# A sum of products by seven instead of eight in the last stage, a new order for the second half, and products of zeros at the start

## The chip, the cores and the metric

The kernel runs on one core of a Trainium2 chip. The metric is the device time of one execution in microseconds (us): the median of three timed runs is 601.54 us, from 601.0 to 602.06. A profile of one further execution goes with them.

The engines by their short names: PE (TensorE) multiplies matrices and writes its sums into PSUM; DVE (VectorE), ACT (ScalarE) and POOL (GpSimd) work on tiles in SBUF, the first two also on PSUM; SP's queue issues most transfers (DMA), and ACT's and POOL's queues issue some.

## The reference

Causal attention of 4 batches x 12 heads, 448 tokens, head size 64, and then on its output an MLP with a squared ReLU, 1792 tokens wide in all, from 768 to 2048 and back to 768:

```python
scores = scale * np.matmul(q, k.transpose(0, 1, 3, 2))       # (4, 12, 448, 448)
scores = np.where(np.triu(ones, k=1), -1e9, scores)
attn = softmax(scores)                                       # over the last axis
x = np.matmul(attn, v).transpose(0, 2, 1, 3).reshape(1792, 768)
h = np.maximum(x @ w_in, 0.0)                                # (1792, 2048)
out = h * h @ w_out                                          # (1792, 768)
```

All is float32. The kernel gets that precision from fast products by writing each factor as a high and a low part; each product of blocks is then three matmuls (high x high, high x low, low x high).

## The kernel before

**Attention** goes by pairs of heads (`attention`). Tiles named a... and b... belong to two pairs that take turns: aq, ak are loaded, transposed on DVE to aqt, akt (line 351); PE makes the scores (line 380); DVE masks them and finds the row extremes (line 393), ACT takes the exponentials into ap (line 397), POOL or DVE divides by the sums (lines 406, 408), PE transposes the result (line 422) to apt, and multiplies it with v (line 464).

**The MLP of the first half** of the tokens (896) is done plainly: h products (`h_unit`, lines 662 to 664), the square, o products (`o_unit`, lines 1081 to 1083). They fill PE between the products of attention.

**The MLP of the second half** works on 2x2 blocks with seven products in the place of eight, Winograd's form: the keys are 11, 12, s1 to s4 and 22, and each has a factor of sums and differences on both sides. d_ff is cut into four groups, taken in the order `TURNS = (0, 3, 2, 1)`. For each group there are two h stages (`h_pair(gr, u, ...)`, u = 0, 1; lines 843 to 847) and one o stage (`o_seven`; lines 969 to 971). A stage works on banks of PSUM; a bank is emptied by ACT (line 266, r<-ps) or by DVE as an add into the running sum of the outputs (line 269, sb<-ps,sb and sa<-ps,sa). DVE, ACT and POOL also make the factors of the next stage from h (the `less`, `square` and `factor` steps), among them sums of two SBUF tiles (r<-r,r; g<-r,g). The factors of the weights are derived once per group by `added_up`: loads, scalings, and transfers from POOL's queue that add into the tile in SBUF. Weights that are already split into high and low parts are loaded by line 944 for the o stages (wi<-wo_split) and by line 783 for the h stages.

**The last o stage** (`o_last`) is plain: four blocks, three column groups (d), and for each four products, so that nothing is left to add up afterwards; the last group's h stages are plain in their last step as well (`plain`). Each output block of 448 tokens is transposed on DVE and stored (lines 1019, 1024); the very last one by PE (`finish`, lines 1046 to 1061), which begins when PE has ended its last product.

**The order.** All instructions are first recorded as operations in a list, with the tiles they take and give back. `PLACES`, a table of base-36 numbers, gives each operation its place in the program and which engine does it where there is a choice (number modulo 3). `emit` then issues the operations in that order. A bank of PSUM or a buffer goes to the next operation that asks for one, the one that was given back first by the program's order. So an engine waits where its next instruction, in this order, isn't ready.

Of the kernel before, what the change touches and what calls it, by code (L numbers as in the profile page):

```python
# [130 lines left out]
def kernel(  # L131
# [85 lines left out]
    def tiles(nm, n, shape, dtype, pool=const):  # L217
        return [pool.tile(shape, dtype, name=f"{nm}{i}") for i in range(n)]

    early = ExitStack()  # L220
# [5 lines left out]
    x_t = tiles("x", NA, [P, 2, S], F32R)  # L226
# [15 lines left out]
    NX = 9  # L242
    wide = wi_t.rearrange("p i c f -> p (i c f)")
# [46 lines left out]
    vs = {}  # L290

    def attention(s, n, at):
# [74 lines left out]
        def softmax(chunks, at):  # L367
# [7 lines left out]
            def scores():  # L375
                for c in chunks:
# [7 lines left out]
            plan.op(at, [(PE, 0.16 + sum(2 * CW[c] / 2400 + 0.01 for c in chunks), scores)],  # L384
                    [(nm, "qt"), (nm, "kt")] + [(nm, "kd")] * any(c in FIRST for c in chunks), holds, take=holds,
                    clear=[(nm, "p", c) for c in chunks], lag=spare(0.6))
# [201 lines left out]
    def piece(rank, kind, gr, a, ch, after):  # L588
# [96 lines left out]
    x7 = {}  # L685
# [144 lines left out]

    def h_pair(gr, u, W, rank, step, plain):

# [4 lines left out]
        def product(key, b, begin):  # L837
            nonlocal rank
            ps, w = bank[b], W[key]
            for c in range(CB):  # L840
                def go(c=c):
# [7 lines left out]
                plan.op(rank, [(PE, 3 * t_mm(S), go)],  # L849
                        [(w, 0), (w, 1)] + [(("x7", OTHER[key], c), i) for i in range(2)], [ps],  # L850
                        take=ps if begin and c == 0 else None, drop=[w])
# [30 lines left out]
        factor("11", "11", plain)  # L882
# [10 lines left out]
        factor("22", "u3", plain)  # L893
# [4 lines left out]
        factor("21", "21", plain)  # L898
# [4 lines left out]
        if plain:  # L903
            factor("12", "12", True)
            return rank
# [18 lines left out]
    O_BANK = {"11": "a", "12": "a", "s3": "d", "s1": "c", "s2": "b", "22": "d", "s4": "c"}  # L924
    O_ENDS = ("12", "s2", "22", "s4")
# [3 lines left out]
    def o_parts(gr, rank, last):  # L929

        W, Z, gate = {}, {}, list(ahead)

        def at(key, u):
            return rank + (last - rank) * (SEVEN.index(key) + u / 2) / 7
# [4 lines left out]
        for m, key in enumerate(("11", "12", "22") if gr != TURNS[-1] else ("11", "12", "21", "22")):  # L939
# [7 lines left out]
        for u in range(2):  # L947
# [8 lines left out]
            if gr != TURNS[-1]:  # L956
                added_up(rank, CH, source, done, lambda t: t, True)
# [48 lines left out]
    def o_last(W, rank, step):  # L1006

        for k in ("11", "21", "12", "22"):
            i, j = k
            for d in range(CB):  # L1010
                ps, a = Hold("ps", "os"), o_sum(k, d)
                rank = o_product(ps, [(W[i + m, u], g7[TURNS[-1], m + j, u]) for m in "12" for u in range(2)],
                                 d, True, True, rank, step)
                if (k, d) == ("22", CB - 1):
                    finish(ps, a, d, rank)
                    continue
                plan.op(rank, [on_dve(S, a, lambda ps=ps: ps.t[:, :S], a, ALU.add)], [ps], [("sum", k, d)], drop=[ps])
                h = Hold("f", "tr")
                plan.op(rank, [(DVE, t_dve(S) + 0.05, lambda h=h, a=a: nc.vector.transpose(h.t, a()))],
                        [("sum", k, d)], [h], take=h)  # L1020
                row, col = T + (int(j) - 1) * S, (int(i) - 1) * CH + d * P
                for s in range(P // SQ):
                    def go(eng, h=h, s=s, row=row, col=col):
                        return lambda: eng.dma_start(
                            out=out[row:row + S, col + s * SQ:col + (s + 1) * SQ].rearrange(
                                "(b p) d -> p b d", p=SQ),
                            in_=h.t[s * SQ:(s + 1) * SQ].rearrange("p (b d) -> p b d", d=SQ))
# [331 lines left out]
```

## Time and profile before

| what | value |
|---|---|
| median of three runs | 601.54 us (601.0 to 602.06) |
| the profiled execution | 601.9 us |
| its span | 599.8 us, mean granted clock 0.995 |
| PE busy | 582.2 us (97%), 3718 instructions |
| DVE busy | 454.8 us (76%), 1077 instructions |
| ACT busy | 351.7 us (59%), 893 instructions |
| POOL busy | 274.5 us (46%), 378 instructions |
| matmuls of the last o stage | 144, each 128x448 |

The span is from the first to the last instruction of the program; the execution's own time lies 2.1 us above it. The trace counts a matmul as busy from its start to its modelled end, so that consecutive ones overlap (a matmul of 448 columns has a length of 0.36 us and follows the one before after about 0.2 us). The granted clock is given in shares of TensorE's full clock of 2.4 GHz.

### The profile page before, as it was taken

The page shows a single profiled execution, that of the slowest core. Times are in us where ns is not written, and L with a number is a line of the kernel's source. Part 1 is how long each engine was busy: PE and PEld are TensorE (multiplying, and loading weights), DVE is VectorE, ACT ScalarE, POOL GpSimd, SP SyncE. Part 2 cuts the span into 40 slices and gives each one's busy share as a digit, 9 for nine tenths or more (in the row PEclk, how much of TensorE's full clock was granted, in tenths as well). Part 3 has the DMA queues.
Part 4 walks back from the last instruction along what each step waited for, and adds up shares of the span by engine and source line. Part 5 has one row for each costly group of instructions (what it writes and reads, how often), then busy time and mean ns, then how long its engine had stood idle before and what let it go on. Part 6 is the DMA issues. An engine that isn't in the chain of part 4 may idle for free.

```text
span 599.8 us, 11359 instructions
## 1 busy us (share of the span) xinstructions
PE 582.2 (97%) x3718; PEld 510.0 (85%) x3718; DVE 454.8 (76%) x1077; ACT 351.7 (59%) x893; POOL 274.5 (46%) x378
## 2 busy tenths in 40 slices
PE   3899999999999999999999999999999999999997
PEld 2577778798988998988889889999999999999996
DVE  5999998688966898897798658577638758776674
ACT  3899987776756853767457442247565645633310
POOL 2566652243135352333224453654766566756310
PEclk9899999999999999999999999999999999999999
DMA  8888534999888987995899699867877766773556
GB/s 148 188 174 203 141 65 111 259 275 315 225 249 248 267 221 171 298 288 154 222 294 309 219 294 277 252 195 175 234 159 172 149 142 144 168 174 60 162 97 103
DMA packets 190650, 119.99 MB, mean 200 GB/s; under 512 B 126016, under 2 KB 178560, under 8 KB 190592
## 3 DMA queue, kind: packets, MB, share of 16 engines
q1 hardware_dynamic: 169488, 107.99, 64.4%
q0 software_dynamic: 6912, 9.44, 10.2%
q10 hardware_dynamic: 14192, 1.85, 1.9%
q8 instruction: 29, 0.48, 0.4%
q14 instruction: 29, 0.24, 0.1%
HBM read 80.71 MB, written 38.54 MB: 199 GB/s over the span
## 4 chain that ended last, share of the span: by engine, by line
PE 91%; ACT 3%; DMA 3%; DVE 1%; SPq 1%; issue 0%; POOL 0%; ACTq 0%
PE ps L1081 7%; PE ps L662 7%; PE ps L1083 7%; PE ps L1082 7%; PE ps L464 6%; PE ps L663 6%; PE ps L664 6%; PE ps L847 6%; PE ps L845 6%; PE ps L843 6%; PE ps L971 6%; PE ps L969 6%; PE ps L970 6%; PE ps L422 6%; PE ps L380 5%; ACT bp L397 1%
## 5 line engine op out<-in xcount | busy, mean ns | idle before, releaser
L266 ACT ACTIVATE words<-words 128x384 f32<-128x384 f32 (+3 forms) x128 | 73.6, 596 | 35.1 <-DVE words L269 11.4
L1081 PE MATMUL ps<-wo,g 128*128 128x384 f32 x224 | 77.3, 345 | 0.0
L393 DVE CUSTOM_DVE_ANT_0 ps<-ps,mask 128x64 f32<-128x64 f32 (+6 forms) x168 | 68.0, 444 | 11.1 <-PE ps L380 9.7
L1083 PE MATMUL ps<-wo,g 128*128 128x384 f32 x224 | 75.1, 335 | 0.0
L1082 PE MATMUL ps<-wo,g 128*128 128x384 f32 x224 | 75.1, 335 | 0.0
L397 ACT ACTIVATE ap<-ps,mx 128x256 f32<-128x256 f32 (+6 forms) x126 | 58.8, 479 | 26.4 <-DVE mx L393 25.5
L662 PE MATMUL ps<-x,wi 128*128 128x448 f32 x192 | 73.7, 384 | 0.0
L663 PE MATMUL ps<-x,wi 128*128 128x448 f32 x192 | 70.2, 365 | 0.0
L664 PE MATMUL ps<-x,wi 128*128 128x448 f32 x192 | 70.2, 365 | 0.0
L406 POOL TENSOR_SCALAR ap<-ap,asm 128x256 f32<-128x256 f32 (+6 forms) x80 | 43.0, 555 | 46.1 <-DVE asm L499 20.6
L970 PE MATMUL ps<-g,wi 128*128 128x448 f32 x153 | 56.0, 366 | 0.0
L971 PE MATMUL ps<-g,wi 128*128 128x448 f32 x153 | 56.0, 366 | 0.0
L969 PE MATMUL ps<-g,wi 128*128 128x448 f32 x153 | 56.0, 366 | 0.0
L273 POOL TENSOR_TENSOR wi<-words,wi 128x384 fp32r<-128x384 f32 (+1 forms) x38 | 45.7, 1227 | 21.4 <-ACT wi L266 20.6
L845 PE MATMUL ps<-x,wi 128*128 128x448 f32 x150 | 55.0, 367 | 0.0
L847 PE MATMUL ps<-x,wi 128*128 128x448 f32 x150 | 55.0, 367 | 0.0
L843 PE MATMUL ps<-x,wi 128*128 128x448 f32 x150 | 54.9, 366 | 0.0
L266 ACT ACTIVATE r<-ps 128x448 f32<-128x448 f32 x56 | 30.1, 542 | 35.5 <-PE ps L847 18.1
L269 DVE TENSOR_TENSOR g<-r,g 128x448 fp32r<-128x448 f32 x54 | 37.4, 703 | 11.1 <-ACT g L266 7.0
L266 ACT ACTIVATE r<-r 128x448 f32<-128x448 f32 x58 | 32.9, 574 | 17.8 <-DVE r L269 17.1
L1081 PEld LDWEIGHTS ps<-wo,g 128*128 128x128 f32 x224 | 42.1, 188 | 1.0 <-issue 0.4
L266 ACT ACTIVATE wi<-words 128x384 fp32r<-128x384 f32 (+1 forms) x53 | 28.5, 545 | 24.6 <-PE ps L970 8.5
(158 smaller groups left out, 1470.4 us busy)
## 6 DMA issues: line engine op xcount, KB each, us to landing
words<-in_moe_w_in_dram SPq DMA_DIRECT2D x24, 512.0 KB, 5.5
words<-in_moe_w_out_dram SPq DMA_DIRECT2D x32, 384.0 KB, 3.8
wo_split<-wo SPq DMA_DIRECT2D x26, 384.0 KB, 4.5
wi<-wo_split SPq DMA_DIRECT2D x22, 384.0 KB, 3.6
wo_whole<-words SPq DMA_DIRECT2D x32, 192.0 KB, 3.5
wi_split<-wi SPq DMA_DIRECT2D x24, 256.0 KB, 3.7
v<-in_v_dram SPq DMA_DIRECT2D x24, 192.0 KB, 4.0
wi_whole<-words SPq DMA_DIRECT2D x18, 256.0 KB, 4.0
```

Source lines behind the costliest of these rows:

```text
L266: return (ACT, t_act(n, psum, more), lambda: nc.scalar.activation(dst(), src(), func, **kw))
L662: nc.tensor.matmul(o, w[:, 0], x[:, 0], start=c == 0, stop=False)
L663: nc.tensor.matmul(o, w[:, 0], x[:, 1], start=False, stop=False)
L664: nc.tensor.matmul(o, w[:, 1], x[:, 0], start=False, stop=c == NP - 1)
L845: nc.tensor.matmul(o, w.t[:, 0, c], x[:, 1], start=False, stop=False, skip_group_check=True)
L847: nc.tensor.matmul(o, w.t[:, 1, c], x[:, 0], start=False, stop=c == CB - 1, skip_group_check=True)
L969: nc.tensor.matmul(o, w.t[:, 0, d], g.t[:, 0], start=start, stop=False, skip_group_check=True)
L970: nc.tensor.matmul(o, w.t[:, 0, d], g.t[:, 1], start=False, stop=False, skip_group_check=True)
L971: nc.tensor.matmul(o, w.t[:, 1, d], g.t[:, 0], start=False, stop=stop, skip_group_check=True)
L1081: nc.tensor.matmul(res(), g[:, 0], w[:, 0], start=f == 0, stop=False)
L1082: nc.tensor.matmul(res(), g[:, 0], w[:, 1], start=False, stop=False)
L1083: nc.tensor.matmul(res(), g[:, 1], w[:, 0], start=False, stop=f == GF - 1)
```

## The change

1. `o_last` makes the last o stage by the seven keys too (`O_LAST`): for each column group 7 keys x 2 halves x 3 matmuls, 126 in all. The results of keys that belong to more than one block are added to more than one running sum: DVE adds from PSUM 21 times in this stage, where it was 12. The last group's weights are now derived by `added_up` (on POOL's queue), and its h stages draw up the factors t1 to t4 as the others do (`plain` is gone).
2. Both h stages of the last group now come before the second-last o stage, and buffers that held the x factors are lent to the g factors and the weights when the last h stage is done with them (`lent_x`).
3. One x tile is set to zero at the start of DVE's queue, and `warmed` issues products of it whose result nobody reads: 15 ahead of the first scores, 7 and 3 among the first transposes.
4. `PLACES` is new. Apart from the zero products, the order of the first half is what it was; from the end of attention on, it is another.

On PE at the start, where akt, aqt, bkt, bqt are the transposed inputs, ap the probabilities of the first pair and x11 the zero tile. Before:

```order
L380 MATMUL ps0_113<-akt_69,aqt_68 64x320 x2
L380 MATMUL ps1_114<-akt_69,aqt_68 64x256 x2
...
L380 MATMUL ps6_119<-bkt_139,bqt_138 64x448 x2
L380 MATMUL ps7_120<-bkt_139,bqt_138 64x384 x2
L380 MATMUL ps7_120<-bkt_139,bqt_138 64x64 x2
L422 MATMUL ps0_113<-ident_64,ap_71 128x128 x4
L422 MATMUL ps2_115<-ident_64,ap_71 128x128 x4
L422 MATMUL ps3_116<-ident_64,ap_71 128x128 x4
```

After:

```order
L307 MATMUL ps0_114<-x11_72 128x448 x15
L398 MATMUL ps1_115<-akt_82,aqt_81 64x320 x2
...
L398 MATMUL ps0_114<-bkt_140,bqt_139 64x384 x2
L398 MATMUL ps0_114<-bkt_140,bqt_139 64x64 x2
L307 MATMUL ps1_115<-x11_72 128x448 x7
L440 MATMUL ps3_117<-ident_77,ap_84 128x128 x4
L307 MATMUL ps4_118<-x11_72 128x448 x3
L440 MATMUL ps2_116<-ident_77,ap_84 128x128 x4
L440 MATMUL ps1_115<-ident_77,ap_84 128x128 x4
```

The products of the zero tile stand ahead of the first scores, behind the second pair's scores, and between the first and the second group of transposes.

On PE in the second half, where h products (into ps banks, from x and weights wi) and o products (from g) interleave. Before, the h stage's bank ps2, between one sum and the next:

```order
L847 MATMUL ps2_115<-x2_8_3924,wi_91 128x448
L843 MATMUL ps7_120<-x2_81,wi_91 128x448
L845 MATMUL ps7_120<-x2_81,wi_91 128x448
L847 MATMUL ps7_120<-x2_81,wi_91 128x448
L843 MATMUL ps3_116<-x4_83,wi_91 128x448
L845 MATMUL ps3_116<-x4_83,wi_91 128x448
L847 MATMUL ps3_116<-x4_83,wi_91 128x448
L843 MATMUL ps2_115<-x6_85,wi_91 128x448
```

After, bank ps4 at the same stage of the program:

```order
L870 MATMUL ps6_120<-x7_68,wi_92 128x448
L866 MATMUL ps4_118<-x2_5_3947,wi_92 128x448
L868 MATMUL ps4_118<-x2_5_3947,wi_92 128x448
L870 MATMUL ps4_118<-x2_5_3947,wi_92 128x448
L866 MATMUL ps6_120<-x8_69,wi_92 128x448
L868 MATMUL ps6_120<-x8_69,wi_92 128x448
L870 MATMUL ps6_120<-x8_69,wi_92 128x448
L991 MATMUL ps4_118<-g3_96,w3_4368 128x448
```

Before, ps2 is used again seven products after the start of the last one of the old sum; after the change, ps4 is used again four products after.

On DVE at the end of the program, where sb5, sb8, sb9, sb10 and sb11 are running sums of output blocks and ps the banks. Before:

```order
L269 TENSOR_TENSOR sb5_4315<-ps5_118,sb5_4315 128x448
L1019 STREAM_TRANSPOSE words_96<-sb5_4315 128x448
L269 TENSOR_TENSOR sb9_4319<-ps2_115,sb9_4319 128x448
L1019 STREAM_TRANSPOSE words_96<-sb9_4319 128x448
L269 TENSOR_TENSOR sb10_4320<-ps3_116,sb10_4320 128x448
L1019 STREAM_TRANSPOSE words_96<-sb10_4320 128x448
L269 TENSOR_TENSOR sb11_4321<-ps0_113,sb11_4321 128x192
L269 TENSOR_TENSOR sb11_4321<-ps0_113,sb11_4321 128x256
```

After:

```order
L277 TENSOR_TENSOR sb11_4389<-ps4_118,sb11_4389 128x448
L277 TENSOR_TENSOR sb11_4389<-ps5_119,sb11_4389 128x448
L1052 STREAM_TRANSPOSE words_97<-sb11_4389 128x448
L277 TENSOR_TENSOR sb8_4386<-ps2_116,sb8_4386 128x448
L277 TENSOR_TENSOR sb5_4383<-ps4_118,sb5_4383 128x448
L1052 STREAM_TRANSPOSE words_97<-sb5_4383 128x448
L277 TENSOR_TENSOR sb8_4386<-ps5_119,sb8_4386 128x256
L277 TENSOR_TENSOR sb8_4386<-ps5_119,sb8_4386 128x192
```

The last block (sb11 before, sb8 after) is in two parts for `finish`; after the change another block's add and transpose (sb5) stand right ahead of these, and the larger part is first.

The diff, cut to its core; of the table one line stands for all:

```diff
+    x_t = tiles("x", NA, [P, 2, S], F32R)
+    zero = x_t[-1][:, 0]
...
+    lent_x = dict(zip(
+        [(key, i) for key in ("11", "21", "t3", "t1", "t2", "t4", "22") for i in range(CB)],
...
+    WARM = (15, (7, 3))
+    def warmed(rank, n, after):
+        ps = Hold("ps", "mm")
+        def go():
+            for i in range(n):
+                nc.tensor.matmul(ps.t[:, :S], zero[:, :P], zero, start=True, stop=True)
+        plan.op(rank, [(PE, n * t_mm(S) * (1 if after else 2), go)], [(("x", NA - 1), i) for i in range(2)], [ps], after, take=ps, drop=[ps])
...
+        if n == 0:
+            warmed(at - 20, WARM[0], ())
         for chunks in groups:
             softmax(chunks, at)
             at += 2.0
+        if n == 0:
+            for m in WARM[1]:
+                warmed(at + 100, m, started[:3])
...
-            if (a % 2, ch) != (0, 1) or gr == TURNS[-1]:
+            if (a % 2, ch) != (0, 1):
...
-    def h_pair(gr, u, W, rank, step, plain):
+    def h_pair(gr, u, W, rank, step):
...
-        if plain:
-            factor("12", "12", True)
-            return rank
         less("11", "12", "11")
         factor("t1", "11", True)
...
+    O_LAST = {"11": ("a", "11"), "12": ("b", "11"), "s2": ("a", "12"), "s1": ("c", "22"),
+              "s3": ("a", "22"), "s4": ("c", "12"), "22": ("a", "21")}
...
-        for m, key in enumerate(("11", "12", "22") if gr != TURNS[-1] else ("11", "12", "21", "22")):
+        for m, key in enumerate(("11", "12", "22")):
...
-            if gr != TURNS[-1]:
-                added_up(rank, CH, source, done, lambda t: t, True)
+            added_up(rank, CH, source, done, lambda t: t, True)
...
     def o_last(W, rank, step):
-        for k in ("11", "21", "12", "22"):
-            i, j = k
-            for d in range(CB):
-                ps, a = Hold("ps", "os"), o_sum(k, d)
-                rank = o_product(ps, [(W[i + m, u], g7[TURNS[-1], m + j, u]) for m in "12" for u in range(2)],
-                                 d, True, True, rank, step)
...
+        bank = {}
+        for d in range(CB):
+            for key, (b, k) in O_LAST.items():
+                begin = key in ("11", "12", "s1")
+                if begin:
+                    bank[b] = Hold("ps", "os")
+                ps, a = bank[b], o_sum(k, d)
+                rank = o_product(ps, [(W[key, u], g7[TURNS[-1], OTHER[key], u]) for u in range(2)],
+                                 d, begin, True, rank, step)
+                if (key, d) == ("22", CB - 1):
+                    finish(ps, k, d, rank)
                     continue
...
+                plan.op(rank, [on_dve(S, a, lambda ps=ps: ps.t[:, :S], a, ALU.add)], [ps], [("sum", k, d)],
+                        drop=[ps] if key in ("12", "22", "s4") else [])
+                if key in ("12", "22", "s3", "s4"):
+                    put_out(k, d, rank)
...
+        early_pair = after == TURNS[-1:]
+        stages += [(a, 0) for a in after] + [(a, 1) for a in after if early_pair]
+        stages += [(gr, None)] + [(a, 1) for a in after if not early_pair]
...
     PLACES = """
-        00f 00l 009 00i 003 00u 00c 00o 006 06r 02l 08o 06l 00x 013 01p 02f 039 03c 03i 03o 02r 02u 01r 026 02x 01x 02i
+        00i 00o 00c 00l 006 00x 00f 00r 009 070 02o 08x 06u 010 016 01s 000 02i 03c 03f 03l 03r 02u 02x 01u 029 030 020
```

## Rows read from the trace of the kernel before

**Rows 1.** The page: busy us and share of each engine; the chain by engine.

```profile
PE 582.2 (97%) x3718; PEld 510.0 (85%) x3718; DVE 454.8 (76%) x1077; ACT 351.7 (59%) x893; POOL 274.5 (46%) x378
...
PE 91%; ACT 3%; DMA 3%; DVE 1%; SPq 1%; issue 0%; POOL 0%; ACTq 0%
```

**Rows 2.** Waits of PE: what it waited for, total us, times, longest.

```profile
PE ps L380 <- DVE aqt L351: 7.4, 1, 7.4
PE ps L422 <- DVE ap L408: 2.4, 1, 2.4
PE ps L422 <- POOL ap L406: 0.8, 1, 0.8
PE ps L380 <- ACT bkt L266: 0.7, 1, 0.7
```

**Rows 3.** Windows: busy us (count) by engine, granted clock, DMA share, GB/s.

```profile
17.00:20.50 3.50, 3.50 (x26) 2.52 (x29) 2.85 (x9) 3.50 (x14) 0.48 (x2) 0.52 0.93 188
60.00:350.00 290.00, 289.90 (x2043) 249.68 (x2037) 236.31 (x626) 195.47 (x525) 111.98 (x159) 1.00 0.82 229
450.00:500.00 50.00, 50.00 (x247) 46.09 (x246) 35.83 (x60) 27.22 (x57) 30.83 (x37) 1.00 0.70 158
503.60:594.70 91.10, 91.07 (x448) 83.72 (x446) 63.87 (x101) 32.19 (x66) 43.17 (x50) 1.00 0.59 132
```

**Rows 4.** Timeline of PE at the start: start us, duration, line, tiles, idle before.

```profile
7.38 3.16 PE L380 MATMUL ps<-akt,aqt 64*64 64x320 f32 x28 [7.38 <-DVE aqt L351]
11.20 1.75 PE L380 MATMUL ps<-bkt,bqt 64*64 64x320 f32 x28 [0.65 <-DVE bqt L351]
...
16.81 2.14 PE L422 MATMUL ps<-ident,ap 128*128 128x128 f32 x10 [0.85 <-POOL ap L406]
18.93 2.51 PE L380 MATMUL ps<-akt,aqt 64*64 64x448 f32 x28
...
33.39 1.43 PE L422 MATMUL ps<-ident,ap 128*128 128x128 f32 x10
```

**Rows 5.** Timeline of DVE at the start.

```profile
9.31 0.43 DVE L393 CUSTOM_DVE_ANT_0 ps<-ps,mask 128x256 f32<-128x256 f32 x1 [0.64 <-PE ps L380]
```

**Rows 6.** Timeline: a last product and the copy that empties its bank.

```profile
558.44 0.37 PE L847 MATMUL ps<-x,wi 128*128 128x448 f32 x1
...
558.85 0.55 ACT L266 ACTIVATE r<-ps 128x448 f32<-128x448 f32 x1 [3.41 <-PE ps L847]
```

**Rows 7.** Line 944, split loads of the o stages: us from issue to landing.

```profile
DMA to landing us min/median/max: 2.8/3.7/5.3
```

**Rows 8.** Groups of DVE from 503.6 to 594.7 us: busy us, mean ns.

```profile
L269 DVE TENSOR_TENSOR sb<-ps,sb 128x448 f32<-128x448 f32 x30 | 18.0, 619 | 12.1 <-PE ps L971 11.9
L269 DVE TENSOR_TENSOR g<-r,g 128x448 fp32r<-128x448 f32 x14 | 9.6, 696 | 3.3 <-ACT g L266 3.3
...
L1019 DVE STREAM_TRANSPOSE words<-sb 128x448 f32<-128x448 f32 x10 | 6.2, 637 | 0.3
L269 DVE TENSOR_TENSOR r<-r,r 128x448 f32<-128x448 f32 x5 | 5.2, 1049 | 0.0
...
L269 DVE TENSOR_TENSOR r<-r,f 128x448 f32<-128x448 f32 x1 | 0.6, 614 | 0.0
```

**Rows 9.** Timeline: adds on POOL and DVE beside each other, and one alone.

```profile
563.18 1.53 POOL L273 TENSOR_TENSOR sb<-sb,sa 128x448 f32<-128x448 f32 x1
...
563.62 1.57 DVE L269 TENSOR_TENSOR r<-r,r 128x448 f32<-128x448 f32 x1
...
569.57 0.62 DVE L269 TENSOR_TENSOR sb<-sb,sa 128x448 f32<-128x448 f32 x1
```

**Rows 10.** Timeline of the tail.

```profile
591.79 3.53 ACTq L1024 DMA_DIRECT2D out_dram<-words  x7
...
594.31 0.36 PE L971 MATMUL ps<-g,wi 128*128 128x448 f32 x1
594.78 0.69 DVE L269 TENSOR_TENSOR sb<-ps,sb 128x192 f32<-128x192 f32 x2 [1.19 <-PE ps L971]
```

More of the change, by code (lines that the diff above doesn't have):

```diff
@@ L218, in tiles @@
         return [pool.tile(shape, dtype, name=f"{nm}{i}") for i in range(n)]
+    x_t = tiles("x", NA, [P, 2, S], F32R)
+    zero = x_t[-1][:, 0]
+    nc.vector.memset(zero.bitcast(F32), 0.0)
     early = ExitStack()
@@ L929, in o_parts @@
     def o_parts(gr, rank, last):
-        W, Z, gate = {}, {}, list(ahead)
+        W, Z, gate, order = {}, {}, list(ahead), tuple(O_LAST) if gr == TURNS[-1] else SEVEN
         def at(key, u):
-            return rank + (last - rank) * (SEVEN.index(key) + u / 2) / 7
+            return rank + (last - rank) * (order.index(key) + u / 2) / 7
         def flat(t):
@@ L1006, in o_last @@
     def o_last(W, rank, step):
-        for k in ("11", "21", "12", "22"):
-            i, j = k
-            for d in range(CB):
-                ps, a = Hold("ps", "os"), o_sum(k, d)
-                rank = o_product(ps, [(W[i + m, u], g7[TURNS[-1], m + j, u]) for m in "12" for u in range(2)],
-                                 d, True, True, rank, step)
-                if (k, d) == ("22", CB - 1):
-                    finish(ps, a, d, rank)
-                    continue
[L1017 to L1027, printed above, removed]
-                    plan.op(rank, [(DMA, 0.6, go(nc.sync), t_dma(S, 128)), (DMA2, 0.6, go(nc.scalar), t_dma(S, 128))], [h], [], drop=[h])
@@ new lines, in o_last, with put_out, go @@
+        return rank
+    def put_out(k, d, rank):
+        i, j = k
+        a, h = o_sum(k, d), Hold("f", "tr")
+        plan.op(rank, [(DVE, t_dve(S) + 0.05, lambda: nc.vector.transpose(h.t, a()))],
+                [("sum", k, d)], [h], take=h)
+        row, col = T + (int(j) - 1) * S, (int(i) - 1) * CH + d * P
+        for s in range(P // SQ):
+            def go(eng, s=s):
+                return lambda: eng.dma_start(
+                    out=out[row:row + S, col + s * SQ:col + (s + 1) * SQ].rearrange(
+                        "(b p) d -> p b d", p=SQ),
+                    in_=h.t[s * SQ:(s + 1) * SQ].rearrange("p (b d) -> p b d", d=SQ))
+            plan.op(rank, [(DMA, 0.6, go(nc.sync), t_dma(S, 128)), (DMA2, 0.6, go(nc.scalar), t_dma(S, 128))], [h], [], drop=[h])
@@ L1046, in turn @@
                     nc.tensor.transpose(turned.t[:n, m - first:m - first + P], a()[:, m:m + n], late["ident"])
[L1047 removed]
+            plan.op(rank, [(PE, 0.22, turn)], [("sum", k, d, first)], [turned], take=turned)
             blocks = [(0, 2, P)] if first == 0 else [(0, 1, P), (1, 1, S - 3 * P)]
@@ L1197 @@
             W = w_parts(gr, u, rank - LEAD, rank + 7 * CB * H_US - LEAD)
-            rank = h_pair(gr, u, W, rank, H_US, last)
+            rank = h_pair(gr, u, W, rank, H_US)
+            if all(v is None for _, v in stages[n + 1:]):
+                for key, ops in used.items():
+                    over(ops, [lent_x[key, i] for i in range(CB)])
     PLACES = """
-        00f 00l 009 00i 003 00u 00c 00o 006 06r 02l 08o 06l 00x 013 01p 02f 039 03c 03i 03o 02r 02u 01r 026 02x 01x 02i
-        03l 03x 020 02o 049 05d 04j 04d 04l 04o 04u 04r 076 07l 06f 06y 07c 086 083 08c 089 09x 0c6 0dr 019 00r 000 01c
```

287 lines of the change are left out of this document (146 added, 141 removed).

## The prediction

> **What bounds the kernel now.** I read the busy shares first. TensorE (PE) works 582.2 of 599.8 us, VectorE (DVE) is the next at 76%, and 91% of the chain that ended last is PE [rows 1]. Shares over a whole span hide stages, so I read the waits of PE next. Of its nine rows the largest are 7.4 us for the first transposed tile, 2.4 us for the first normalised probabilities and 0.8 us for their second half [rows 2]; no other is over 0.7 us. These belong to the start. The stretches tell of the rest: 289.90 busy of 290.00 us from 60 to 350 us, and 91.07 of 91.10 us in the last 450 products, from 503.6 to 594.7 us [rows 3]. From there on the time is the number of products, times the distance from one to the next, plus a tail of 5.5 us after the start of the last one (599.8 - 594.31) [rows 10].
>
> The start is different. From 17 to 20.5 us the granted clock was 0.52, so TensorE was at its 1.2 GHz level, after 2.4 us of waiting for the probabilities [rows 2, 3]. The first 28 products of the scores were slow too: they took 3.16 us where the next 28 of the same shapes took 1.75 us [rows 4].
>
> All sums below are against the profiled execution, whose time is 601.9 us (span 599.8 and 2.1 us around it). It lies 0.36 us above the median of 601.54, which I take off at the end. A difference under 0.2% (1.2 us) can't be told from none.
>
> **The change, part by part.**
>
> *Fewer products.* The last o stage falls from 4 blocks x 3 column groups x 4 pairs x 3 = 144 matmuls to 7 x 3 x 2 x 3 = 126. From 450 to 500 us, 50.00 us held 247 matmuls [rows 3], 0.2024 us each, and nearly all there are 128x448. So 18 x 0.2024 = **-3.64 us**. All of it is on the path as long as PE stays without gaps, and each of the next terms is a way to get one. By the Trainium skill ("TensorE: Matmul & The Clock Gate", Back-to-back issue gap), N columns cost N/2.4 + 2.5 ns, 189 ns here; by that the saving would be 3.40 us. The row has 202 ns; the measurement decides.
>
> *Zero products at the start.* Fifteen are put ahead of the first scores, seven and three among the first transposes. The fifteen need at most 15 x 2 x 0.2024 = 6.1 us, twice the full-speed distance. They wait only for one memset on DVE, the first in its queue; PE was empty until 7.38 us [rows 4], so from about 1.3 us they end near 7.4 us, hidden under the loads. What they can buy: the first scores lost 3.16 - 1.75 = 1.41 us, the ten transposes 2.14 - 1.43 = 0.71 us, the second scores 2.51 - 1.75 = 0.76 us [rows 4], 2.88 us in all. But after the first scores DVE is the engine that works without a pause, and it had waited only 0.64 us for them [rows 5]; so at most 0.64 + 0.71 + 0.76 = 2.1 us arrive. And waits for engines that were not PE's followers stand behind it: 0.7 us for a copy by ACT [rows 2], and DMA, whose busy share was 0.93 here [rows 3]; a gain that arrives there early waits longer. Between 0 and -2.1 I take the row of DVE's own wait, **-0.7 us**, with both ends kept. A loss is possible only if the fifteen end after 7.38 us, a few tenths.
>
> *The new order of the second half: banks.* A PSUM bank is free for a new sum once ACT or DVE has emptied it. One product started at 558.44, ACT's copy started at 558.85 and took 0.55 us [rows 6]: with some 0.05 us to hand over that is 0.41 + 0.55 + 0.05 = 1.01 us from the start of the last product, five products. Before, the tightest reuse behind a copy by ACT has seven starts between (1.42 us). After the change two places have only four, 0.81 us, one of them shown in the section on the change, where ps4 is written, one other bank gets three products, and ps4 is begun anew. Each costs 0.2 us if ACT starts at once, more if ACT has something in front: **+0.4 us** (0 if ACT's hand-over is quicker than the row, 1.5 if each finds one 0.55 us copy ahead).
>
> *The new order: weights.* The last stage's factors must now be derived (on POOL's queue, accumulating transfers), and split loads come into buffers that other products free late. A split load landed in 2.8 to 5.3 us, 3.7 in the middle [rows 7]. From a buffer's last use to its next one I count at least 28 products before (5.66 us) and 22 and 25 after, at two places (4.45 and 5.06 us). With 0.3 us for the issue, the median fits; the longest landing would miss by 1.3 and 0.7 us. **+0.1 us**, with 0 to 1.9.
>
> *DVE's load.* The seven-product form adds sums from PSUM: 21 where there were 12, and adds of two SBUF tiles for the factors. In the last 450 products DVE had 101 instructions in the trace (103 in the order) and was busy 63.87 us of 91.10 [rows 3]. In the new order I count 132 there: 62 that read PSUM, 59 that read two SBUF tiles, 11 transposes. From the groups of that stretch, PSUM adds take 0.619 us; the eight two-SBUF groups, from 14 of 0.696 down to single ones, hold 41 instructions and 31.1 us, 0.759 each [rows 8]; the transposes 0.637. So 62 x 0.619 + 59 x 0.759 + 11 x 0.64 = 90.2 us, where PE's time is 91.1 us. The engine goes from 70% to 99% by this count (before, 67.5 us of such durations showed as 63.87 busy, so perhaps 94%). PE does not wait for DVE's mean but for its queue: a bank whose add is late. Before, that queue had 27 us of slack here; now a burst of POOL work can make it late. I take one late two-SBUF instruction of the longer kind, 1.5 against 0.7 us, on the path: **+0.8 us** (0 to 7; rival A).
>
> The price of 0.759 is not a constant. A DVE add of two SBUF tiles that ran beside a POOL add of 1.53 us took 1.57 us, one beside no POOL work 0.62 us [rows 9]. The Trainium skill ("GPSIMD Engine Reference", Key points) says that GpSimd shares its SBUF interfaces with VectorE and contends with instructions that have two SBUF inputs; this trace agrees by the 1.57 against 0.62 us.
>
> In the same 450 products POOL's tensor adds go from 20 to 26 by the order.
>
> *The tail.* Before, the last product is followed by two DVE adds (0.69 us), transposes, copies and stores [rows 10]. In the new order DVE has an add and a transpose (0.62 + 0.64 us, [rows 8]) due just ahead of them, ends them some 0.15 to 0.2 us late, adds the larger part first, and ACT's queue has three more stores of about 0.5 us (seven took 3.53 us) in front of its last one [rows 10]. **+0.45 us** (0.2 if ACT's queue is empty in time, 1.2 if two stores stand in front).
>
> *At nothing:* the POOL and ACT instructions added (16 and 29), since POOL is busy 43.17 and ACT 32.19 us of those 91.10 [rows 3]; and the first half's order, which is unchanged apart from the zero products.
>
> The sum: -3.64 - 0.7 + 0.4 + 0.1 + 0.8 + 0.45 = -2.59; 601.9 - 2.59 = 599.3; less 0.36, **598.9 us**.
>
> **The rivals.**
>
> A. *DVE becomes the bound of the last 450 products* (slower). Mechanism: more POOL adds lie beside more DVE adds of two SBUF tiles, these lengthen, DVE's queue falls behind and PE waits for banks. Place: from the last pair's factors on. It eats the whole gain at a mean of 0.83 us (38.4 + 59 x 0.83 + 7.0 = 94.4, 3.3 us late); at 0.85 to 0.9 the stretch takes 95.6 to 98.5 us, 4.5 to 7.4 us late in the place of 0.8: 602.6 to 605.5, about 604. It decides from 0.85. For it: r<-r,r already has a mean of 1.049 [rows 8]. Against: the other groups stay near 0.7, and instructions overlap a little. Chance 0.13.
>
> B. *Tight places cost more.* Weights at their worst (+1.9) or banks and tail at theirs (+1.1, +0.75) instead of the middle: 598.9 + 1.8 to + 2.4 = 600.7 to 601.3, about 601.0: no difference. For it: the landings spread up to 5.3 us; against: the DMA share there is 0.59 [rows 3]. Chance 0.16.
>
> C. *The zero products buy nothing*, since the loads and ACT set the pace of the first 55 us: 598.9 + 0.7 = 599.6. That part of the change then doesn't do what it is there for. For it: the waits of [rows 2]. Chance 0.12.
>
> D. *The start pays in full and nothing new waits*: -3.64 - 2.1 + 0.2 + 0.2 = -5.3, 596.2. For it: the slow products stood in PE's own queue, and what follows them waits for PE. The Trainium skill ("TensorE: Matmul & The Clock Gate", Part 1) says that the slow level is the default and that activity releases it; the 3.16 against 1.75 us agrees. Against: the DMA share of 0.93 there. Chance 0.15.
>
> **How the numbers follow.** The forecast has 0.44, from 597.4 to 600.3. The range takes D nearly whole and ends at A's lower edge: 595.8 to 602.6, which leaves out most of A and a little of D's far side. Faster by over 0.2% (under 600.34): forecast 0.43, C 0.11, D 0.15, a piece of B 0.01: 0.70. Within 0.2%: most of B and the rest of C, with the weak half of A: 0.17. Slower (over 602.74): A, 0.13.
>
> **What would show it.** Right: the last o stage with 126 products 0.20 us apart; no granted clock near 0.5 between 7.4 and 20.5 us, and a shorter wait of PE for the first probabilities; waits of PE for ACT of 0.2 us at the two banks; DVE busy 90 to 95% of the last 450 products with a two-SBUF mean under 0.8 us; 5.9 us from the start of the last product to the end. Wrong: a PE wait for DVE's adds of several us in the last 90 us (A), waits for split weights (B), the same clock as before or the same arrival at 55 us (C), over 1.5 us gained by 55 us (D).

## The result, and the profile after

The changed kernel took 609.0 us, median of 4 runs (607.74 to 609.77), beside 601.57 for the kernel before: a ratio of 1.0122, interval 1.0109 to 1.0135. It is 7.4 us slower where 2.6 us faster was forecast, and outside the range. The profiled execution took 609.15 us, with a span of 607.4.

The page of the profile after, the busy shares and the chain by engine:

```profile
PE 587.8 (97%) x3725; PEld 512.3 (84%) x3725; DVE 476.3 (78%) x1093; ACT 363.0 (60%) x921; POOL 293.7 (48%) x394
...
PE 84%; DVE 5%; DMA 4%; ACT 4%; issue 2%; SPq 0%; POOLq 0%; POOL 0%; ACTq 0%; DVEq 0%
```

PE has 18 products less to do in the last stage (and the 25 zero products more at the start) and is busy longer than before [rows 1]; DVE has gone from 1% to 5% of the chain. The largest waits of PE:

```profile
PE ps L991 <- DVE sb L277: 5.4, 2, 3.0
PE ps L307 <- DVE x L222: 1.4, 1, 1.4
PE ps L398 <- DVE aqt L369: 1.3, 1, 1.3
...
PE ps L991 <- DMA wi<-wo_split: 1.0, 2, 0.6
```

Against [rows 2] the waits at the start are smaller, and there is a new one at the top: the o products (line 991, where 969 was) waited twice for DVE's adds, 5.4 us. It isn't at the start. The timeline of PE around the two places:

```profile
564.46 0.37 PE L993 MATMUL ps<-g,wi 128*128 128x448 f32 x1
567.82 0.47 PE L991 MATMUL ps<-g,x 128*128 128x448 f32 x1 [3.00 <-DVE sb L277]
...
568.80 0.57 PE L991 MATMUL ps<-g,x 128*128 128x448 f32 x1
569.17 0.57 PE L992 MATMUL ps<-g,x 128*128 128x448 f32 x1
...
578.74 0.71 PE L991 MATMUL ps<-x,x 128*128 128x448 f32 x1 [2.36 <-DVE sb L277]
```

And four stretches (columns as in [rows 3]):

```profile
17.00:20.50 3.50, 2.69 (x35) 1.69 (x33) 3.31 (x12) 3.45 (x13) 1.26 (x3) 1.00 1.06 186
567.80:572.00 4.20, 4.18 (x13) 3.75 (x14) 2.72 (x5) 1.35 (x3) 1.12 (x2) 0.59 0.06 12
578.70:582.10 3.40, 3.36 (x10) 3.03 (x11) 1.71 (x4) 0.00 (x0) 0.00 (x0) 0.54 0.02 5
509.90:601.50 91.60, 85.62 (x402) 77.27 (x400) 76.23 (x115) 37.85 (x80) 51.33 (x57) 0.96 0.64 138
```

Each wait is followed by products 0.37 us apart, twice the usual distance, at a granted clock of 0.59 and 0.54: TensorE fell to its 1.2 GHz level after 3.0 and 2.4 us without a product, for 8 products 0.37 us apart (and a few between the levels) after each. The first row answers to the one of [rows 3] with 0.52: at the start the clock is now 1.00.

Why was DVE late? DVE and POOL ahead of the first wait:

```profile
561.50 3.19 DVE L277 TENSOR_TENSOR sb<-sb,sa 128x448 f32<-128x448 f32 x1
...
561.65 2.29 POOL L281 TENSOR_TENSOR x<-words,x 128x384 fp32r<-128x384 f32 x2
...
564.19 1.61 POOL L281 TENSOR_TENSOR wi<-words,wi 128x384 fp32r<-128x384 f32 x1
...
564.61 2.62 DVE L277 TENSOR_TENSOR g<-r,g 128x448 fp32r<-128x448 f32 x1
565.51 1.23 POOL L281 TENSOR_TENSOR wi<-f,wi 128x384 fp32r<-128x384 f32 x1
567.16 0.61 DVE L277 TENSOR_TENSOR sb<-ps,sb 128x448 f32<-128x448 f32 x1
```

and ahead of the second:

```profile
572.43 1.31 POOL L281 TENSOR_TENSOR wi<-words,wi 128x384 fp32r<-128x384 f32 x1
...
572.65 3.80 DVE L277 TENSOR_TENSOR x<-r,x 128x448 fp32r<-128x448 f32 x1
...
573.41 2.55 POOL L281 TENSOR_TENSOR sb<-sb,sa 128x448 f32<-128x448 f32 x2
...
577.45 0.61 DVE L277 TENSOR_TENSOR sb<-ps,sb 128x448 f32<-128x448 f32 x1
```

Three DVE instructions that read two SBUF tiles took 3.19, 2.62 and 3.80 us, where the usual is 0.61. The last two began while POOL was at work on two sources, and ended 0.49 us after the end of POOL's whole unbroken stretch: 567.23 against 565.51 + 1.23 = 566.74, and 576.45 against 573.41 + 2.55 = 575.96. (The first ended 564.69, 0.75 us after POOL's two and half a microsecond after 564.19, where POOL's next one began: it got in at a change.) The adds from PSUM that free banks stood behind them, at 567.16 and 577.45, and PE began again 0.05 us after the end of the first of these (567.77) and 0.15 us after the second add of the other pair.

The end of the stretch is not always what counts. In the kernel before, an add got in between POOL's third and fourth instruction of a stretch:

```profile
542.97 2.98 POOL L273 TENSOR_TENSOR wi<-words,wi 128x384 fp32r<-128x384 f32 x3
...
545.16 1.28 DVE L269 TENSOR_TENSOR g<-r,g 128x448 fp32r<-128x448 f32 x1
545.91 1.41 POOL L273 TENSOR_TENSOR wi<-f,wi 128x384 fp32r<-128x384 f32 x1
```

It ended at 546.44, 0.49 us after 545.95, and POOL's fourth took 1.41 us. From 350 us to the end of the changed kernel, 22 adds of two SBUF tiles began while POOL was at two-source work, and each ended 0.48 to 0.51 us after the end of one of POOL's instructions: of 7 that had another of POOL's directly behind, four got in before it, and three, the two of 2.62 and 3.80 us among them, waited for it as well. What decides this isn't shown. An add thus waited at most until some half a microsecond behind POOL's stretch (0.75 us for the first of the three above), and at times less.

The difference put together, along PE, from the starts of the products. The same first product with apt after 333 us starts at 333.28 before and 332.48 after: -0.80. The 18 products: -3.64. The two waits: the gaps of 3.36 and 2.73 us less the usual 0.20, 5.7. The slow products: 3.1. Split weights that came late, at 488 and 531 us, 1.5, and a gap at 486 us that the view of waits doesn't name (PE began 0.09 us after ACT had copied a derived weight), 0.3: 1.8, with the late product behind each. Two banks, at 466 and 544 us: 0.7. A wait for DVE's g at 358 us: 0.4. The tail (607.4 - 601.48 = 5.92, where it was 5.49): 0.4. Sum: +7.7; the spans differ by 7.6.

### The profile page after: what moved, and what is told of

Read it like the earlier page. It is cut to its first block, busy times and chain, and to the rows that moved or that the text cites. A ratio compares the mean times of both kernels' runs of the same rounds, so it can differ in the third digit from the quotient of the medians.

```text
span 607.4 us, 11457 instructions
## 1 busy us (share of the span) xinstructions
PE 587.8 (97%) x3725; PEld 512.3 (84%) x3725; DVE 476.3 (78%) x1093; ACT 363.0 (60%) x921; POOL 293.7 (48%) x394
## 4 chain that ended last, share of the span: by engine, by line
PE 84%; DVE 5%; DMA 4%; ACT 4%; issue 2%; SPq 0%; POOLq 0%; POOL 0%; ACTq 0%; DVEq 0%
PE ps L482 7%; PE ps L1114 6%; PE ps L685 6%; PE ps L1116 6%; PE ps L1115 6%; PE ps L686 6%; PE ps L687 6%; PE ps L866 5%; PE ps L868 5%; PE ps L870 5%; PE ps L440 5%; PE ps L398 5%; PE ps L991 4%; PE ps L992 4%; PE ps L993 4%
## 5 line engine op out<-in xcount | busy, mean ns | idle before, releaser
L274 ACT ACTIVATE words<-words 128x384 f32<-128x384 f32 (+3 forms) x139 | 79.1, 589 | 45.3 <-DVE words L277 13.3
L685 PE MATMUL ps<-x,wi 128*128 128x448 f32 x192 | 73.7, 384 | 0.0
L686 PE MATMUL ps<-x,wi 128*128 128x448 f32 x192 | 70.2, 366 | 0.0
L687 PE MATMUL ps<-x,wi 128*128 128x448 f32 x192 | 70.2, 365 | 0.0
L866 PE MATMUL ps<-x,wi 128*128 128x448 f32 x156 | 57.2, 367 | 0.1
L868 PE MATMUL ps<-x,wi 128*128 128x448 f32 x156 | 57.2, 367 | 0.0
L870 PE MATMUL ps<-x,wi 128*128 128x448 f32 x156 | 57.2, 366 | 0.0
L281 POOL TENSOR_TENSOR wi<-words,wi 128x384 fp32r<-128x384 f32 (+1 forms) x39 | 47.7, 1226 | 18.4 <-ACT wi L274 17.7
L274 ACT ACTIVATE wi<-words 128x384 fp32r<-128x384 f32 (+1 forms) x58 | 30.9, 540 | 37.9 <-PE ps L993 11.8
L277 DVE TENSOR_TENSOR g<-r,g 128x448 fp32r<-128x448 f32 x54 | 41.9, 780 | 7.7 <-ACT g L274 7.5
L1114 PEld LDWEIGHTS ps<-wo,g 128*128 128x128 f32 x224 | 42.1, 188 | 1.0 <-issue 0.4
L1116 PEld LDWEIGHTS ps<-wo,g 128*128 128x128 f32 x224 | 42.1, 188 | 0.6 <-DVE g L277 0.6
L277 DVE TENSOR_TENSOR sb<-ps,sb 128x448 f32<-128x448 f32 (+2 forms) x55 | 32.1, 607 | 13.3 <-PE ps L993 12.9
L1115 PEld LDWEIGHTS ps<-wo,g 128*128 128x128 f32 x224 | 42.1, 188 | 0.4
L991 PE MATMUL ps<-g,wi 128*128 128x448 f32 x108 | 39.7, 368 | 1.0 <-DMA wi<-wo_split 1.0
```

Source lines behind the costliest of these rows:

```text
L274: return (ACT, t_act(n, psum, more), lambda: nc.scalar.activation(dst(), src(), func, **kw))
L277: return (DVE, t_dve(n) + more, lambda: nc.vector.tensor_tensor(out=dst(), in0=a(), in1=b(), op=op))
L685: nc.tensor.matmul(o, w[:, 0], x[:, 0], start=c == 0, stop=False)
L686: nc.tensor.matmul(o, w[:, 0], x[:, 1], start=False, stop=False)
L687: nc.tensor.matmul(o, w[:, 1], x[:, 0], start=False, stop=c == NP - 1)
L866: nc.tensor.matmul(o, w.t[:, 0, c], x[:, 0], start=begin and c == 0, stop=False, skip_group_check=True)
```

## The experiments

The order is a table with a place for each operation; most edits put a few operations at other places (in the diffs place: new place) and change nothing else. The theories: **1**, GpSimd's two-source work holds VectorE's adds of two SBUF tiles, and these hold up what stands behind them; **2**, VectorE has too many instructions for the time.

### 1. Adds from PSUM first

```diff
-        codes = [int(x, 36) for x in table.split()]
+        codes = [({3363: 3368.2, 3364: 3368.4, 3411: 3392.5, 3399: 3392.7, 3394: 3408.6, 3396: 3408.3}.get(c // 3, c // 3), c % 3) for c in ...]
```

> The changed kernel, with six instructions of VectorE's queue in another order and nothing else: at two places the adds from PSUM that free a bank for TensorE stand ahead of the adds of two SBUF tiles (the sum of u2 for block 22, the low parts of factors t4, t3 and t4), where they stood behind them. Theory 1 (an add of two SBUF tiles is held up for as long as GpSimd's two-source work lasts, 3.19, 2.62 and 3.80 us in the changed kernel's profile, and the adds from PSUM wait behind it): TensorE's two waits for VectorE, 3.0 and 2.4 us, and the slow clock behind them, some 3 us, go nearly away: 609.0 - 7 to 8.5 = 600.5 to 602. Theory 2 (VectorE has too many instructions for the time, in whatever order): the waits come back a few products later, 607 to 609. VectorE's instruction count is the same.

606.35 us, ratio 1.0084 (1.0071 to 1.0097): a third of the expected gain. The first wait is gone. The second is there, 3.2 us, and 14 products 0.37 us apart behind it. The instruction that met POOL's stretch was now another one of the same kind:

```profile
571.11 1.32 POOL L281 TENSOR_TENSOR wi<-words,wi 128x384 fp32r<-128x384 f32 x1
...
571.51 3.61 DVE L277 TENSOR_TENSOR x<-f,x 128x448 fp32r<-128x448 f32 x1
...
572.10 2.53 POOL L281 TENSOR_TENSOR sb<-sb,sa 128x448 f32<-128x448 f32 x2
```

It ended 575.12, POOL at 574.63: 0.49 us again. The run doesn't decide between the theories; it shows that the hold stays when the order changes and only picks another victim.

### 2. GpSimd with one source

```diff
+        lone[0] = gr in TURNS[-2:]
...
+        return (POOL, t_pool(n, True), (lambda: nc.gpsimd.tensor_scalar(dst(), a(), 1.0, 1.0, op0=ALU.mult, op1=ALU.mult)) if lone[0] else
                 lambda: nc.gpsimd.tensor_tensor(out=dst(), in0=a(), in1=b(), op=op)) + SHARED
```

> The changed kernel, with GpSimd's two-source subtractions and adds of the last two groups' o and h stages replaced by copies of one source (this leaves the low parts of those weight factors and some of the sums out of the computation); VectorE's instructions and their order are the same. Theory 1 (GpSimd's two-source work holds up VectorE's adds of two SBUF tiles): no such add over 1.3 us in the last 100 us, where there were 3.19, 2.62 and 3.80, TensorE's waits for VectorE there go from 5.4 us to under 1, and the time is 600 to 602. Theory 2 (too many instructions on VectorE): at least half of the 5.4 us stays, 605 to 609.

601.07 us, ratio 0.9991 (0.9982 to 1.0). PE has no wait for DVE in the o products any more, and the clock is 1.00 there. Two adds of two SBUF tiles took 1.82 us (at 527.40) and 1.79 us, more than the 1.3 expected. The last 91 us:

```profile
502.50:593.60 91.10, 90.45 (x442) 82.38 (x440) 75.61 (x127) 41.19 (x88) 42.41 (x61) 1.00 0.71 153
```

Theory 2 falls with this row: DVE had 127 instructions in 91.1 us and was busy 75.61, as busy as in the changed kernel (76.23 of 91.60, above), and no o product waited for it. Not the load, but three long holds with bank-freeing adds behind them made the time.

The theory's words "two-source work" are too narrow, though. The add of 1.79 us was held by one-source work in the same way:

```profile
564.70 0.83 POOL L280 TENSOR_SCALAR wi<-words 128x384 fp32r<-128x384 f32 x1
564.76 1.79 DVE L277 TENSOR_TENSOR g<-r,g 128x448 fp32r<-128x448 f32 x1
565.18 0.88 POOL L280 TENSOR_SCALAR sb<-sb 128x448 f32<-128x448 f32 x1
```

It ended at 566.55, POOL at 566.06: 0.49 us again. In the changed kernel, too, all 20 adds of two SBUF tiles that began beside POOL's one-source tensor work after 350 us ended 0.40 to 0.48 us after one of its instructions. What this experiment took away is the length of the holds: POOL is busy 42.41 us here, where it was 51.33 of 91.60.

### 3. Two of GpSimd's adds on VectorE

```diff
+        codes = [(c // 3, {3427: 0, 3436: 0}.get(c // 3, c % 3)) for c in ...]
```

> The changed kernel, with two of GpSimd's adds of two SBUF tiles (u2 into blocks 22 and 12, second column group) on VectorE instead, at the same places of the order; VectorE so gets two instructions more. Theory 1, as it stands after the first runs (a VectorE add of two SBUF tiles that meets GpSimd at two-source work ends 0.5 us after the end of GpSimd's unbroken stretch): the stretch from 572.4 to 576.0 us ends after its first 1.3 us, the 3.80 us add takes 1.3 to 1.8 us, TensorE's second wait shrinks from 2.4 to under 1 us, and the clock need not fall there: 609.0 - 2 to - 4 = 605 to 607. Theory 2 (VectorE has too many instructions): two more make it slower, 609.5 to 611.

606.78 us, ratio 1.0097 (1.0079 to 1.0114): by the median 2.2 less than the changed kernel, with two instructions more on DVE, as theory 1 had it. (One of its four runs took 609.41, and the two intervals overlap a little: that it isn't slower is shown, how much faster it is isn't.) The first wait, not touched, is there (2.4 us); the second is gone, and one of 1.0 us has come at 584 us, behind an add that DVE got, which was itself held for 1.34 us. The second place:

```profile
572.00 1.30 POOL L281 TENSOR_TENSOR wi<-words,wi 128x384 fp32r<-128x384 f32 x1
...
572.76 1.03 DVE L277 TENSOR_TENSOR x<-r,x 128x448 fp32r<-128x448 f32 x1
```

POOL's stretch now ends at 573.30, DVE's add at 573.79 (+0.49): 1.03 us in the place of 3.80, with the same instruction at the same place.

### 4. Both edits

```diff
+        codes = [({3363: 3368.2, 3364: 3368.4, 3411: 3392.5, 3399: 3392.7, 3394: 3417.2, 3396: 3417.3, 3413: 3408.3}.get(c // 3, c // 3),
+                  {3427: 0, 3436: 0}.get(c // 3, c % 3)) for c in ...]
```

> The changed kernel with both edits: the two adds of u2 on VectorE, and at two places of VectorE's order the adds from PSUM ahead of the adds of two SBUF tiles (the low parts of t3 and t4 behind the last stage's first five adds from PSUM). Theory 1: no wait of TensorE for VectorE over 1 us in the last 100 us and no slow clock there; what stays of the changed kernel's losses are the waits for split weights and banks, 2.4 us, and the tail: 609.0 - 9.0 = 600.0, from 599 to 601.5. Theory 2: 605 or more.

603.37 us, ratio 1.0034 (1.0023 to 1.0045). No slow clock, but waits for DVE of 0.4 and 1.5 us stay, 2.4 us with the products behind them: the time lies above theory 1's 601.5 and below theory 2's 605. DVE has no pause from 563 to 581 us here, and ahead of the adds that free banks stand transposes for the output and, before the wait of 1.5 us, one more held add (1.32 us). So in this one stretch DVE's own queue counts as well.

### 5. One add earlier, transposes later

```diff
+        codes = [({..., 3436: 3403.5, 3418: 3426.2, 3435: 3445.2, 3442: 3458.2, ...}.get(c // 3, c // 3),
+                  {3427: 0}.get(c // 3, c % 3)) for c in ...]
```

> The kernel with both edits, developed further: of the two adds of u2 one (block 12) goes back to GpSimd, but earlier, behind the fourth-last weight factor, where VectorE is at adds from PSUM; the other (block 22) stays on VectorE; and the transposes of the first three finished blocks, with their stores, stand behind the next adds from PSUM. Theory 1 refined (adds from PSUM aren't held up by GpSimd, so GpSimd's work beside them costs nothing; what is left in the kernel with both edits is VectorE's own queue from 563 to 581 us, without a pause): TensorE's waits for VectorE of 0.4 and 1.5 us, 2.2 us with the products after them, shrink under 0.5: 603.4 - 1.7 to - 2.2 = 601.2 to 601.7. If adds from PSUM are held up as well: GpSimd's earlier add lengthens them and the time is 603 or more.

601.2 us, ratio 0.9999 (0.9988 to 1.001), as expected: 7.8 us under the changed kernel, and no faster than the kernel before, with some twenty operations (stores among them) at other places. POOL's add now runs beside DVE's adds from PSUM:

```profile
567.75 2.20 DVE L277 TENSOR_TENSOR sb<-ps,sb 128x448 f32<-128x448 f32 x4
...
568.97 1.17 POOL L281 TENSOR_TENSOR sb<-sb,sa 128x448 f32<-128x448 f32 x1 [2.71 <-DVE sb L277]
```

Four adds from PSUM take 2.20 us in a row, one beginning every 0.53 us, the last two of them beside POOL's two-source add: adds with one source in PSUM are not held. In the last 91 us DVE is busier than in any other version and PE has few gaps:

```profile
502.00:593.00 91.00, 90.48 (x441) 81.98 (x439) 79.27 (x128) 41.57 (x89) 54.03 (x61) 1.00 0.71 153
```

In this profiled execution (600.66 us) seven small gaps between 358 and 577 us still take 2.5 us together and the longer tail 0.4: most of the 3.64 us of the products.

### 6. Two products between the banks

```diff
+        codes = [({... as in 5, 3259: 3267.5, 2848: 2827.5}.get(c // 3, c // 3), ...
```

> The kernel with one add early and the first transposes late (601.2), with two products moved in TensorE's order: at the two places where a bank was begun anew only four products after its last one, another product now stands between, so that seven are. By the row of an ACT copy (0.41 + 0.55 + 0.05 = 1.01 us, five products) both waits should go: gaps of 0.49 and 0.38 us there, 0.66 us over the 0.20 with the products behind them, and the time is 600.5 to 600.7. If another wait stands behind these (a later bank, a weight): less than 0.3 us, 600.9 to 601.2.

601.23 us, ratio 0.9994 (0.9983 to 1.0006). Both gaps are gone from the trace, and the time is the same within the intervals, which couldn't tell 0.66 us either. In the profiled execution a wait for the split weight at 532 us has grown:

```profile
PE ps L991 <- DMA wi<-wo_split: 1.0, 1, 1.0
```

PE waits 1.0 us for it, where in the twin it had a gap of 0.42 in all. But the load also took longer, 5.75 us from issue to landing where it was 4.79, and this wait is anything from 0 (experiment 1) to 1.0 us in the versions here. That a weight stands behind the banks, as the rival of the expectation had it, fits this one trace; it isn't shown that it took what the banks gave.

### 7. Without the zero products, and the kernel before with them

```diff
-            for i in range(n):
+            for i in range(0):
                 nc.tensor.matmul(ps.t[:, :S], zero[:, :P], zero, start=True, stop=True)
```

> The changed kernel without the 25 products of the zero tile (its memset stays). The traces of both kernels put the gain of these at 0.8 us by 337 us. Theory 1 (that gain is carried to the end): 609.0 + 0.8 = 609.8. Rival (it is taken back before the end, because the second half is held by other engines): 609.0, within 0.3.

607.23 us, ratio 1.0093 (1.008 to 1.0106): 1.8 us faster, where 0.8 slower was expected. At 333 us it is 1.1 us behind the changed kernel (333.56 against 332.48); it makes that up in the last stages, where its waits for DVE are 4.1 in the place of 5.4 us and 9 products are 0.37 us apart instead of 16. Why the holds came out shorter (2.89 and 3.39 us for two of them, where they were 3.19 and 3.80) isn't shown; the engines meet at other moments.

> The kernel with both edits, without the 25 products of the zero tile. Where the last stages no longer wait, the gain at the start should stay: 0.8 to 1.1 us slower than the kernel with both edits (601). Rival: the zero products cost more than they give (without them the changed kernel ran 1.8 us faster, not 0.8 slower as expected): 1 to 2 us faster.

603.92 us, ratio 1.0041 (1.0026 to 1.0055): 0.55 more than with them, intervals that overlap, so neither is shown.

> The same kernel without the 25 zero products. The kernel before gained 0.8 us by them. If nothing waits in the last stages any more, it is that much slower without them: 0.6 to 1.0 us more than its twin. If the waits there still depend on when each engine arrives: any difference between - 1 and + 1.

600.86 us, ratio 0.9992 (0.9983 to 1.0001): 0.3 less than with them, no difference that these runs can tell.

In the kernel before, the zero products were put in the first operation of the scores and of the transposes:

```diff
             def scores():
+                for i in range(15 if n == 0 and chunks[0] == ORDER[0] else 0):
+                    nc.tensor.matmul(pss[0].t[:, :S], zero[:, :P], zero, start=True, stop=True)
...
```

> The kernel before with the zero products alone: 15 ahead of the first scores, 7 and 3 ahead of the first two groups of transposes (there they take the banks of the transposes), and the memset of the tile. If the gain of 0.8 us of the changed kernel's start is theirs: 601.57 - 0.8 = 600.8, at most 1.0 less. If the rest of the change made it: 601.6.

605.65 us, ratio 1.0066 (1.0054 to 1.0078). A miss of the experiment's own: `ORDER[0]` is in the second operation that PE gets, so the fifteen stood between two halves of the scores:

```profile
7.51 1.77 PE L384 MATMUL ps<-akt,aqt 64*64 64x320 f32 x16 [7.51 <-DVE aqt L353]
9.21 4.75 PE L379 MATMUL ps<-x 128*128 128x448 f32 x15
13.89 0.99 PE L384 MATMUL ps<-akt,aqt 64*64 64x448 f32 x12
```

On the path, 4.75 us of zero products cost 4.1 us. With `ORDER[3]` and bank 2 (and 7 and 3 the other way round):

> The kernel before with the zero products, now really ahead of the first scores (in the first attempt 15 stood between the first and the second half of them, on the path, 4.75 us) and 7 and 3 ahead of the first two groups of transposes. If the 0.8 us of the changed kernel's start are theirs: 600.8, from 600.4 to 601.2. If they are taken back by what the first 55 us wait for: 601.6.

600.74 us, ratio 0.9988 (0.9979 to 0.9996): 0.8 us faster, as expected, and the only version here that is faster than the kernel before with an interval clear of 1.

## Why the prediction was wrong, by its steps

**The step that failed** is DVE's load, the term of +0.8 us (0 to 7). It priced "one late two-SBUF instruction of the longer kind, 1.5 against 0.7 us", from [rows 9]. Those rows held the mechanism: the DVE add ended 563.62 + 1.57 = 565.19, POOL's 563.18 + 1.53 = 564.71, 0.48 us apart. Read as a price ("1.57 us beside POOL") it gave a mean; read as a wait (it ends 0.5 us after POOL's work, at worst after a whole unbroken stretch) it asks how long POOL's stretches are in the new order and what stands on DVE behind each. At the second place the table put a weight and two sums on POOL in a row, and VectorE's bank-freeing adds behind a factor's low part. The waits measured 5.7 us where the term had 0.8.

**Rival A** named the engines, the cause and the place, with a chance of 0.13, and still was too small: 602.6 to 605.5. Its mechanism was half right. The load itself came as counted. The last 450 products of the changed kernel:

```profile
499.86:601.85 101.99, 96.00 (x451) 86.47 (x449) 85.73 (x130) 42.64 (x90) 57.35 (x64) 0.97 0.64 138
```

DVE had 130 instructions in the trace and was busy 85.73 us (counted: 132, and 90.2 or "perhaps 94%", which is 85.6 of 91.1), and its 60 instructions of two SBUF tiles took 0.838 us on average, short of the 0.85 from which A decides. By A's own sum PE would have been 3.7 us late (38.4 + 59 x 0.838 + 7.0 = 94.8 against 91.1); it waited 5.7 us and lost 3.1 to the clock behind that, and experiment 2 shows as many DVE instructions without such a wait. It isn't a mean that decides.

**The other rivals.** B's condition for the weights came, inside a larger loss; its upper end of +2.4 doesn't follow from its terms, which give 1.8 and 1.85. C and D fall with the 0.8 us that the start gained: neither nothing nor over 1.5.

**What no step had** is the clock: each of the two waits (3.0 and 2.4 us) in the middle of the program cost 1.5 to 1.7 us again in slow products, 3.1 in all. The prediction looked at the clock only at the start.

**Fewer products**, -3.64: the order has them, and gaps apart the products stay 0.20 us apart. Right.

**The start**, -0.7: measured -0.8 at 52 us (the same product started at 52.58 before and 51.79 after) and still at 333 us. Right in size and, by these rows, in mechanism:

```profile
1.40 4.97 PE L307 MATMUL ps<-x 128*128 128x448 f32 x15 [1.40 <-DVE x L222]
7.71 1.75 PE L398 MATMUL ps<-akt,aqt 64*64 64x320 f32 x28 [1.34 <-DVE aqt L369]
...
14.86 0.63 PE L440 MATMUL ps<-ident,ap 128*128 128x128 f32 x4 [0.76 <-DVE ap L426]
...
16.34 1.31 PE L440 MATMUL ps<-ident,ap 128*128 128x128 f32 x10 [0.24 <-POOL ap L424]
18.46 1.84 PE L398 MATMUL ps<-akt,aqt 64*64 64x448 f32 x28 [0.81 <-DVE akt L369]
...
24.22 0.60 PE L355 MATMUL ps<-ident,rows 112*128 112x112 f32 x4 [0.88 <-DMA rows<-in_q_dram]
```

The first scores take 1.75 us in the place of 3.16, the second 1.84 in the place of 2.51 [rows 4], and there is a wait for DMA (0.88 us at 24.22), as was said. But the arrival isn't the same each time: against 333.28 in the kernel before, the versions with zero products ahead of the first scores came there between 332.5 and 333.4, those without between 333.0 and 333.7. The firmer sign is the second attempt in experiment 7, 0.8 us over 11 runs (0.2 to 1.3 by its interval).

**Banks**, +0.4: measured 0.7 with the products behind, 0.2 to 0.3 each for the wait. The row behind it held to 0.01 us:

```profile
543.45 0.37 PE L870 MATMUL ps<-x,wi 128*128 128x448 f32 x1
...
543.86 0.54 ACT L274 ACTIVATE r<-ps 128x448 f32<-128x448 f32 x1 [0.82 <-PE ps L870]
...
544.45 0.47 PE L991 MATMUL ps<-g,w 128*128 128x448 f32 x1
```

0.41 + 0.54 + 0.05 = 1.00 us from the start of the last product to the new one. Experiment 6 took both gaps away without a gain that its runs could tell.

**Weights**, +0.1 (0 to 1.9): 1.8 us, the far end, of which split loads are 1.5. At 531 us the count was right: the load was issued at 525.91, 4.7 us before its use, and took 5.34. The wait at 488 us was not at such a place: issued 6.2 us before its use, that load took 6.66. So the landings weren't those of before, and the misses that the prediction worked out from them (1.3 and 0.7 us; its terms without a hand-over give 1.15 and 0.54) rested on a longest landing of 5.3. In the changed kernel, issue to landing of these loads, against [rows 7]:

```profile
DMA to landing us min/median/max: 3.0/4.7/9.3
```

The middle is 4.7 us where it was 3.7, and the longest 9.3 where it was 5.3: the prediction used landings of before for a kernel that has eight more accumulating transfers of 192 KB on POOL's queue (56, where there were 48). Whether these make the landings late isn't shown.

**The tail**, +0.45: 0.43, the size by other parts than forecast. DVE's add and transpose stand just ahead of the finish, as the order showed:

```profile
601.32 0.65 DVE L1052 STREAM_TRANSPOSE words<-sb 128x448 f32<-128x448 f32 x1
601.48 0.37 PE L993 MATMUL ps<-x,wi 128*128 128x448 f32 x1
601.98 0.69 DVE L277 TENSOR_TENSOR sb<-ps,sb 128x256 f32<-128x256 f32 x2
...
603.25 0.48 DVE L1088 COPY words<-ps 128x128 f32<-128x128 f32 x2 [0.58 <-issue]
```

But the last two adds start 0.50 us after the last product's start, where it was 0.47 [rows 10]: they are 0.03 us late, not 0.15 to 0.2. The rest comes behind them: with the larger part first, DVE's copies of the smaller part begin 1.77 us after the last product's start, where it was 1.36 (595.67 - 594.31), and ACT's copy of the larger part begins at 603.56, behind three stores that ACT's queue issues until 603.46.

## What to carry to other kernels

In these traces an add of two SBUF tiles on VectorE isn't slowed by GpSimd's tensor work, it waits for it: count how long GpSimd's unbroken stretches are as the most that such an add can wait, and put adds from PSUM, which don't wait, beside them and ahead of the adds of two SBUF tiles. When fewer products are bought with more work on the engines around, price the longest hold on the engine that frees the banks, not its mean load, and add what the clock takes after a long wait. A wait removed is worth what the next one behind it leaves: even the best new order here gave 3.6 us of products away to small waits and a longer tail.

What stays open: why the changed kernel is faster without its zero products, when an add gets in between two of GpSimd's instructions, and why the wait for the split weight at 531 us is 0 to 1.0 us from version to version.

## What the runs showed of the hardware

- In the changed kernel from 350 us on, 42 DVE adds of two SBUF tiles began while POOL was at tensor work. The 22 beside two-source work ended 0.48 to 0.51 us after the end of one of POOL's instructions, the 20 beside one-source work 0.40 to 0.48 us after. Where POOL's next instruction followed at once, some got in before it and some waited for it too: 3.80 us behind three instructions in a row was the longest. Experiments 1 and 3 show 0.49 us again, for adds of 3.61 and 1.03 us.
- Adds with one source in PSUM were not held: the 32 of them that began beside two-source work took 0.61 us on average and 0.63 at most, those elsewhere 0.60.
- TensorE fell to 1.2 GHz after waits of 2.36, 2.41, 2.44, 3.00 and 3.24 us in the middle of a full stretch, for 8 to 14 products 0.37 us apart; after waits of 1.50 and 1.62 us it did not.
